# Half of the dense weights narrowed in place during the dense layers, lanes of 108 in the router, and thresholds on ScalarE

## The chip, the cores and the metric

The kernel runs on one core of a Trainium2 chip. Its engines are TensorE (PE, with its weight loads PEld), VectorE (DVE), ScalarE (ACT), GpSimd (Pool) and SyncE (SP), which issues most DMAs. Each engine runs its own instructions in the order written and waits for semaphores. The metric is the device time of one execution in microseconds, lower is better. The kernel is built with every order fixed in the code.

## What is computed

Three stages in a row: an attention that keeps only the scores within `tau` of the row's largest, a mixture of eight experts with one expert per token, and two dense layers whose weights come in float64.

```python
# attention: batch 4, heads 8, 576 tokens, head size 64
scores = scale * q @ k.T
scores = where(scores >= max(scores) - tau, scores, -1e9)
attn = softmax(scores); x = attn @ v                # 2304 x 512 after the heads are joined
# experts: 8 of them, 512 -> 1024 -> 512
logits = x @ w_gate; e = argmax(logits); gate_w = softmax(logits)[e]
eom = sigmoid(x @ w_output_gate)[e]
y[mask of e] = gate_w * eom * (relu(x[mask] @ w1[e]) @ w2[e])
# dense layers: 512 -> 2048 -> 512; w_in and w_out are float64
h = y @ w_in; g = maximum(0.01 * h, h); out = g @ w_out
```

## The kernel before

**Attention** (0 to about 341 us). The work is 16 pairs of heads by nine score tiles of 128 rows x 576. For a tile, PE multiplies (L443), DVE takes the row maximum (`rowmax`, L452), a subtraction gives the threshold `th` = `ntau` - `nm` (L456, on DVE or Pool, as the planner chose), ACT makes the exponential `e` (L462), and DVE masks it, `em` (L470); PE transposes `em` (L499), ACT copies that (`eta`, L228), and PE multiplies by the values (L578). At a pair's start Pool splits the next keys and queries into a high and a low part: two CASTs (L290) and two subtractions (L295). A planner (`pl.add`) lists every step with its cost, what it waits for and a priority made of the tile's number and a weight (`st.w_th` and others); the order that comes out is fixed for each engine.

**Router.** After each batch of tokens, gate logits give the expert of a token (one hot `oh`) and its rank in the expert (`rk`). From rank and expert a table of tokens per expert is inverted on PE: a one-hot row of the rank's low part (`lo`, in lanes of 128) against `sides`, made of the rank's high part (J = 4 groups) and the token number. After the third of four batches `choose` takes the expert with most tokens so far (the star) and gathers its first PRE = 216 tokens; their first layer (L1460) runs at 341 to 354 us, while the last batch is routed. Then `tables` makes the gather list of the largest expert, `fits` sets a flag (L1116), DVE goes on to the lists of the others and the starts in the output, and every engine branches past a spare program for experts that don't fit (L1982, L1983).

**Expert windows** (364 to 623 us). The star's second layer, then the eight experts in order of size, each with a capacity from `CAPS`. All operands are split in a high and a low part and multiplied in three passes. For each, SP loads a quarter of w1 or w2 (512 KB) into one of four buffers `raw` (L1592), ACT casts the high part (L1559), DVE or Pool subtracts for the low part (L1564), PE multiplies (L1661 and L1702), ACT and DVE make the hidden values (L1669, L1675). Tokens come by gathers of 128 rows (L1621) and transposes (L1630).

**Narrowing.** Meanwhile `narrow` turns the float64 weights of the dense layers into float32, in 32 pieces of 128 x 512: a load into `dw`, three integer steps on DVE (L1323, L1329, L1335), an absolute value on ACT (L1341), a fourth DVE step (L1345), and a store of the piece, `cv`, to the DRAM tensor `wf` (L1350).

**Dense layers** (from 623 us). Tokens run in five chunks of up to 512, and within a chunk f = 0 to 15 over blocks of 128 hidden values: `h2` (12 matmuls, L1836) and `out` (12 matmuls, L1862). `act_t` and `act_g` (L1843, L1847) make g in `tg`, which lies in the `dw` buffers, and two steps split it. In the first chunk the weights come back from `wf` as 16 loads of 512 KB into `raw` (L1752) and are split by ACT and by DVE or Pool; later chunks find them in place.

## Time and profile before

| | |
|---|---|
| three runs | 1031.01, 1031.69 (median), 1036.69 us |
| profiled execution | 1034.34 us, its span 1032.6 us |
| PE busy | 982.6 us (95%) |
| DVE, ACT, Pool busy | 658.5, 498.0, 260.2 us |
| moved by DMA | 122.22 MB |

The span is what the profile covers, from the first to the last instruction; the device's time lies a little above it. The profile's numbers are of that one execution. "Busy" is what an engine spends inside instructions. The granted clock is the TensorE clock in tenths or hundredths of full speed; 0.50 and 1.00 are its two levels, 1.2 and 2.4 GHz. An idle time stands with the instruction that ended it, with the releaser behind the arrow.

### The profile page before, as it was taken

How to read it: one execution, taken by the hardware profiler on the slowest of the kernel's cores; microseconds unless marked ns; L12 is line 12 of the kernel's file. 1: busy time of each engine (PE TensorE's matmuls, PEld its weight loads, DVE VectorE, ACT ScalarE, POOL GpSimd, SP SyncE). 2: the span in 40 equal slices, each digit the busy share in tenths (PEclk: the TensorE clock that was granted, in tenths of full speed). 3: DMA queues.
4: the chain of work that ended last, by engine and by line, in shares of the span. 5: the costliest groups of instructions: out<-in, count | busy, mean ns of one | idle time of the engine just before them, and what ended most of it. 6: DMA issues, size and time to landing. Idle time of an engine off the chain costs nothing. (4 is left out here: it accounts for less than half of the span.)

```text
span 1032.6 us, 17029 instructions
## 1 busy us (share of the span) xinstructions
PE 982.6 (95%) x6126; PEld 836.8 (81%) x6126; DVE 658.5 (64%) x1279; ACT 498.0 (48%) x944; POOL 260.2 (25%) x328
## 2 busy tenths in 40 slices
PE   6999999999999799899999999999999999999994
PEld 6777767767776699789999997888888888888884
DVE  7888988898889558998888886533223222322321
ACT  6777767767766255544554644423222322322321
POOL 3533223323211244464337532000100100100000
PEclk9999999999999989899999999999999999999997
DMA  5432423431312597887989877200200200100000
GB/s 140 127 86 71 129 59 85 127 73 41 103 25 96 166 260 261 296 269 241 324 298 320 289 241 232 83 1 12 70 1 1 81 1 1 42 20 1 11 31 22
DMA packets 66876, 122.22 MB, mean 118 GB/s; under 512 B 15776, under 2 KB 33184, under 8 KB 66272
## 3 DMA queue, kind: packets, MB, share of 16 engines
q1 hardware_dynamic: 60368, 100.43, 30.5%
q0 software_dynamic: 6416, 20.63, 7.3%
q8 instruction: 50, 0.82, 0.3%
q14 instruction: 42, 0.34, 0.2%
HBM read 88.39 MB, written 23.31 MB: 108 GB/s over the span
## 5 line engine op out<-in xcount | busy, mean ns | idle before, releaser
L1862 PE MATMUL ps<-arena 128*128 128x512 f32 x864 | 207.4, 390 | 2.3 <-ACT arena L1559 2.3
L1836 PE MATMUL ps<-arena 128*128 128x512 f32 (+1 forms) x960 | 208.1, 368 | 0.0
L1836 PEld LDWEIGHTS ps<-arena 128*128 128x128 f32 x960 | 168.7, 188 | 30.8
L1862 PEld LDWEIGHTS ps<-arena 128*128 128x128 f32 x864 | 161.3, 188 | 35.7 <-ACT arena L1559 2.7
L1847 DVE TENSOR_TENSOR dw<-ps,dw 128x512 f32<-128x512 f32 (+1 forms) x80 | 50.9, 638 | 160.7 <-ACT dw L1843 160.6
L1702 PE MATMUL ps<-arena 128*128 128x216 f32 (+7 forms) x864 | 129.8, 309 | 3.8 <-ACT arena L1669 2.2
L1843 ACT ACTIVATE dw<-ps 128x512 f32<-128x512 f32 (+1 forms) x80 | 44.4, 556 | 183.4 <-PE ps L1836 183.4
L1661 PE MATMUL ps<-arena 128*128 128x400 f32 (+7 forms) x768 | 117.9, 313 | 10.7 <-DVE arena L1675 4.1
L1702 PEld LDWEIGHTS ps<-arena 128*128 128x128 f32 x864 | 124.0, 194 | 4.8 <-ACT arena L1669 2.5
L1661 PEld LDWEIGHTS ps<-arena 128*128 128x128 f32 x768 | 113.9, 194 | 13.6 <-DVE arena L1675 5.1
L452 DVE TENSOR_REDUCE nm<-ps 128x1 f32<-128x576 f32 x144 | 107.0, 753 | 22.4 <-PE ps L443 21.1
L470 DVE SCALAR_TENSOR_TENSOR em<-ps,th,e 128x576 f32<-128x576 f32 x144 | 115.1, 811 | 4.6 <-ACT e L462 2.3
L462 ACT ACTIVATE e<-ps,nm 128x576 f32<-128x576 f32 x144 | 105.7, 749 | 17.0 <-DVE nm L452 12.2
L1891 POOL DMA_INDIRECT out_dram<-sm,oidx x18 | 18.0, 999 | 367.4 <-ACT sm L1885 334.2
L1564 DVE TENSOR_TENSOR arena<-dw,arena 128x512 fp32r<-128x512 f32 (+1 forms) x80 | 52.0, 650 | 91.6 <-PE ps L1862 75.8
L443 PE MATMUL ps<-k,qt 128*128 128x288 f32 x512 | 101.6, 326 | 7.2 <-DVE em L470 6.0
L228 ACT COPY eta<-ps 128x512 f32<-128x512 f32 (+1 forms) x159 | 86.2, 545 | 42.3 <-PE ps L499 41.0
L1559 ACT CAST arena<-raw 128x1024 fp32r<-128x1024 f32 x82 | 84.7, 1048 | 43.1 <-DMA raw<-in_moe_w_dram 33.3
L1564 POOL TENSOR_TENSOR arena<-raw,arena 128x1024 fp32r<-128x1024 f32 x30 | 77.0, 2568 | 82.8 <-ACT arena L1559 69.1
L443 PEld LDWEIGHTS ps<-k,qt 128*128 128x128 f32 x512 | 75.8, 196 | 25.0 <-DVE em L470 10.6
L1564 DVE TENSOR_TENSOR arena<-raw,arena 128x1024 fp32r<-128x1024 f32 x54 | 78.2, 1451 | 26.7 <-ACT arena L1559 21.6
L499 PE MATMUL ps<-ident,em 128*128 128x128 f32 x576 | 89.8, 281 | 1.3 <-DVE em L470 0.7
(236 smaller groups left out, 1161.5 us busy)
## 6 DMA issues: line engine op xcount, KB each, us to landing
raw<-in_moe_w_dram SPq DMA_DIRECT2D x72, 512.0 KB
k<-k POOLq DMA_DIRECT2D x30, 304.0 KB
dw<-in_moe_w_in_dram SPq DMA_DIRECT2D x16, 512.0 KB
wf<-cv SPq DMA_DIRECT2D x32, 256.0 KB
dw<-in_moe_w_out_dram SPq DMA_DIRECT2D x16, 512.0 KB
raw<-wf SPq DMA_DIRECT2D x16, 512.0 KB
rk<-in_k_dram SPq DMA_DIRECT2D x16, 256.0 KB
rq<-in_q_dram SPq DMA_DIRECT2D x16, 256.0 KB
```

Source lines behind the costliest of these rows:

```text
L228: nc.scalar.copy(out=out, in_=in_)
L443: nc.tensor.matmul(out=s[:, c, :], lhsT=lhs, rhs=T[kk, P][:, off + c * HALF:off + (c + 1) * HALF], start=(m == 0), stop=(m == 2 * len(ops) ...
L452: nc.vector.tensor_reduce(out=T["nm", n], in_=T["sc", n], axis=AX.XY, op=ALU.max, negate=True)
L462: nc.scalar.activation(out=T["e", n].rearrange("p (a c) -> p a c", a=2), in_=T["sc", n], func=AF.Exp, bias=T["nm", n][:, 0:1], scale=1.0,)
L470: nc.vector.scalar_tensor_tensor(out=T["em", P, t][:, h, :].rearrange("p (a c) -> p a c", a=2), in0=T["sc", n], scalar=T["th", n][:, 0:1], ...
L499: nc.tensor.transpose(out=bank(o)[:, c * 128:(c + 1) * 128], in_=T["em", P, t][:, h, 64 * h + c * 128:64 * h + (c + 1) * 128], identity=ident,
L1559: nc.scalar.copy(out=out, in_=in_)
L1564: (nc.vector if o.eng == "dve" else nc.gpsimd).tensor_tensor(out=out, in0=in0, in1=in1, op=ALU.subtract)
L1661: nc.tensor.matmul(out=bank(o)[:, 0:n], lhsT=w[:, wi, 128 * f:128 * f + 128], rhs=xx[:, xi, c, :], start=(c == 0 and i == 0), stop=(c == K ...
L1702: nc.tensor.matmul(out=bank(first, d)[:, 0:n], lhsT=w[:, wi, k0:k0 + 128], rhs=hx[:, xi, :], start=(f == 0 and i == 0), stop=(f == 7 and i ...
L1836: nc.tensor.matmul(out=bank(o)[:, 0:n], lhsT=w[:, wi, c, 128 * c2:128 * c2 + 128], rhs=y[:, c, 0:n], start=(k == 0), stop=(k == 3 * KD - 1),)
L1862: nc.tensor.matmul(out=bank(first, t), lhsT=g[:, gi, 128 * t:128 * t + 128], rhs=w[:, wi, c2, :], start=(f == 0 and k == 0), stop=(f == FF ...
```

## The change

Five things change.

1. `narrow` stores only the first 16 pieces (EARLY = 4) to `wf`. The other 16 are loaded, narrowed and, by `late`, split straight from `cv` into the weights' place while the dense layers run: an ACT cast (or DVE), and a subtraction on Pool (15) or DVE (1). `tg` moves from `dw` to `raw`, so that the first `act_t` waits for the split of the last early weight.
2. The router counts ranks in lanes of 108 (LANES) and six groups, and makes its entries batch by batch. `choose` inverts the whole table instead of a copy for the star. The lists of the other experts and the starts are made behind the branch, and gathers of later windows wait for the former.
3. The thresholds run on ACT (85 activations) or Pool (59).
4. CAPS[2] goes from 336 to 324, and windows are gathered in blocks of 108 instead of 128 (25 gathers instead of 23).
5. The priorities of attention and router get new values, which gives a new order on all engines.

```diff
+LANES = PRE // 2
-CAPS = [400, 368, 336, 320, 296, 272, 248, 216]
+CAPS = [400, 368, 324, 320, 296, 272, 248, 216]
+EARLY = 4
...
-                (nc.vector if o.eng == "dve" else nc.gpsimd).tensor_tensor(
-                    out=T["th", n], in0=ntau, in1=T["nm", n], op=ALU.subtract
-                )
+                if o.eng == "act":
+                    nc.scalar.activation(out=T["th", n], in_=T["nm", n], func=AF.Identity, bias=ntau[:, 0:1], scale=-1.0)
+                else:
+                    nc.gpsimd.tensor_tensor(out=T["th", n], in0=ntau, in1=T["nm", n], op=ALU.subtract)
...
-            th = pl.add(("dve", "pool"), (0.07, 0.15), thresh, [m], n + st.w_th, label="th")
+            th = pl.add(("act", "pool"), (0.18, 0.15), thresh, [m], n + st.w_th, label="th")
...
-    J = 4
+    J, JW = 6, 4
...
+        entered = self.entries(pl, b, ranked, one_hot, prio)
         if end:
-            return self.tables(pl, ranked, self.last_cum, self.entries(pl, b, b + 1, ranked, one_hot, prio), prio)
+            return self.tables(pl, self.last_cum, entered, prio)
+        self.before += entered
...
         pt = pl.add("dve", 0.6, parts, [ranked], prio, label="en")
+        hi = pl.add("dve" if end else "pool", 0.4, high, [pt], prio, label="en")
+        out = [pl.add("dve", 0.8, low, [pt], prio, label="en")]
...
-        m = pl.add("dve", 2.0, mine, [s, ranked], pr, label="ch")
-        ls = [pl.add("dve", 0.8, lambda o, b=b: low(o, b), [m], pr, label="ch") for b in range(NB)]
-        p = pl.add("pe", 1.0, mm, [*ls, m], pr, acq=[(bk, 1)], label="ch")
+        p = pl.add("pe", 1.0, lambda o: self.inverse(o, 0, 5 * NB, o, 5 * NB), self.before, pr, acq=[(bk, 1)], label="ch")
...
-        a = add("dve", 0.9, fits, [a])
-        a = add("dve", 1.2, lambda o: tokens(o, 1, E), [a])
-        return add("dve", 1.1, starts, [a])
+        self.others, self.starts = lambda o: tokens(o, 1, E), starts
+        return add("dve", 0.9, fits, [a])
...
-def narrow(pl, nc, dw, cv, w_in, w_out, wf, t0, t1):
+def narrow(pl, nc, dw, cv, w_in, w_out, wf, t0, t1, split):
...
-    for i in range(n):
+    for i in range(n_all):
...
+        if i >= n:
+            split(i, e, a, r_cv, lambda B=B: B["c"].bitcast(F32))
+            continue
...
+    others = pl.add("dve", 1.2, R.others, [], -13, at=free, label="tb")
+    starts = pl.add("dve", 1.3, R.starts, [], 5, at=free, label="tb")
...
-            nt = (n + 127) // 128 if r is not None else 0
+            nt = -(-n // LANES) if r is not None else 0
...
-            g = pl.add("pool", 1.1, gather, [], lead - 8, after=[pool_last], acq=[(r_sm, 1)], dma=0.73, label="gather", at=0.0 if a < 2 else free)
+            g = pl.add("pool", 1.1, gather, [others] if r else [], lead - 8, after=[pool_last], acq=[(r_sm, 1)], dma=0.73, label="gather", at=0.0 if a < 2 else free)
...
+    def late(i, e, a, r_cv, src):
...
+        w = late.when(i)
+        b = pl.add(AD, (0.59, 0.45), hiw, [e, O.get(("wh", k - 1)), *(ends if k >= ar.NW else [prev_hi]), *O.get(("hf", k), [])], w + 0.5,
+                   acq=[(r_w, 1)] if k < ar.NW and half_ == 0 else [], label="wh")
+        l = pl.add(("dve", "pool"), (0.74, 1.4), low, [b], w + 0.6, rel=[(r_cv, a)], label="wl")
...
+    late.when = lambda i: t2 + 10.8 * (i // 4) - 20 + 2.7 * (i % 4)
+    wdone = narrow(pl, nc, dw, cv, w_in, w_out, wf, st.w_n0, t2 - st.w_n1, late)
+    for u in range(NE):
...
-            tt = pl.add("act", ev(n)[0], lambda o, a=a, f=act_t: f(o, a), [a], bf + 3, acq=[(r_t, 1)], label="t")
+            tt = pl.add("act", ev(n)[0], lambda o, a=a, f=act_t: f(o, a), [a, O["wv", 2 * NE - 1]], bf + 3, acq=[(r_t, 1)], label="t")
...
-    st.w_s, st.w_m, st.w_th, st.w_x, st.w_kk, st.w_t, st.w_te = -0.39, -0.27, -4.42, -1.71, -7.74, 2.69, -4.82
+    st.w_s, st.w_m, st.w_th, st.w_x, st.w_kk, st.w_t, st.w_te = -0.83, -9.42, -28.19, 3.88, -7.61, 2.26, -14.75
...
-            st.tg = [t.bitcast(F32).rearrange("p f a -> p (f a)").rearrange("p (a f) -> p a f", a=2) for t in st.dw]
+            st.tg = [t.rearrange("p (a f) -> p a f", a=2) for t in st.raw[2:4]]
```

**ACT in attention.** Before, in the early score tiles, ACT's row holds the exponentials `e` (L462), the copies of the transposed tiles (`eta`, `etl`, L228) and a copy for the output (`xu`):

```order
L228 COPY eta<-ps 128x4x128
L462 ACTIVATE e<-ps,nm 128x576 x2
L228 COPY eta<-ps 128x4x128
L462 ACTIVATE e<-ps,nm 128x576
L228 COPY xu_171<-ps 128x288
L228 COPY etl<-ps 128x384
L228 COPY eta<-ps 128x4x128
L462 ACTIVATE e<-ps,nm 128x576
```

After, in about the same place (exponential L467, copies L232), thresholds stand among them:

```order
L461 ACTIVATE th<-nm,ntau 128x1
L467 ACTIVATE e<-ps,nm 128x576
L232 COPY etl<-ps 128x384
L232 COPY eta<-ps 128x4x128
L467 ACTIVATE e<-ps,nm 128x576
L232 COPY eta<-ps 128x4x128
L467 ACTIVATE e<-ps,nm 128x576
L232 COPY eta<-ps 128x4x128
```

The threshold, made by the same subtraction before on DVE or Pool, now stands ahead of an exponential.

**DVE at the branch.** Before, the flag (L1116) is followed by the gather lists of the other experts (L1103 to L1108) and the sums for the starts:

```order
L1116 TENSOR_SCALAR flag<-mcap 128x1
L1103 TENSOR_TENSOR scr<-one,tab 128x224
L1107 TENSOR_REDUCE tk_4651<-scr 128x28
L1108 TENSOR_SCALAR gidx<-tk_4651 128x28
L1120 TENSOR_TENSOR scr<-gt,cnt 128x64
L1121 TENSOR_REDUCE off<-scr 128x8
L1122 TENSOR_SCALAR off<-off 128x8
L1064 TENSOR_TENSOR scr<-one,off 128x64
```

and the branch stands behind these, the first router steps of the last batch's gate, and the first split of a weight (L1564):

```order
L823 TENSOR_TENSOR d<-lg_4557,m 128x40
L833 TENSOR_TENSOR og<-oh,lg_4557 128x40
L835 TENSOR_REDUCE os<-og 128x5
L1564 TENSOR_TENSOR arena<-raw_66,arena 128x1024
L1982 TENSOR_LOAD flag
L1983 COMPARE_AND_BRANCH
```

After, the comparison with the capacities (L1085 to L1089) ends in the flag and the branch:

```order
L1085 TENSOR_TENSOR scr<-one,capr 128x64
L1086 TENSOR_REDUCE cap<-scr 128x8
L1087 TENSOR_TENSOR dcap<-cnt,cap 128x8
L1088 TENSOR_REDUCE mcap<-dcap 128x1
L1089 TENSOR_SCALAR flag<-mcap 128x1
L1991 TENSOR_LOAD flag
L1992 COMPARE_AND_BRANCH
```

The lists of the others and the starts now stand behind the branch, the lists as the first rows there.

**DVE and PE in the first chunk of the dense layers.** Before, DVE's row there holds the activation's second step (`act_g`, L1847), the split of g (L1564 from `dw`) and splits of weights that came back from `wf` (from `raw`):

```order
L1564 TENSOR_TENSOR arena<-dw_4689,arena 128x512
L1847 TENSOR_TENSOR dw_4690<-ps,dw_4690 128x512
L1561 CAST arena<-raw_68 128x1024
L1564 TENSOR_TENSOR arena<-dw_4690,arena 128x512
L1847 TENSOR_TENSOR dw_4689<-ps,dw_4689 128x512
L1564 TENSOR_TENSOR arena<-dw_4689,arena 128x512
L1564 TENSOR_TENSOR arena<-raw_69,arena 128x1024
L1847 TENSOR_TENSOR dw_4690<-ps,dw_4690 128x512
L1564 TENSOR_TENSOR arena<-dw_4690,arena 128x512
```

After, in the first chunk, the same two steps of the activation (L1856, and L1543 from `raw`) stand between the four narrowing steps of the pieces (L1299, L1305, L1311, L1321):

```order
L1299 TENSOR_SCALAR cv_4688<-dw_4686 128x512
L1305 SCALAR_TENSOR_TENSOR cv_4688<-dw_4686,cv_4688 128x512
L1311 SCALAR_TENSOR_TENSOR cv_4688<-dw_4686,cv_4688 128x512
L1856 TENSOR_TENSOR raw_68<-ps,raw_68 128x512
L1321 SCALAR_TENSOR_TENSOR cv_4688<-dw_4686,cv_4688 128x512
L1543 TENSOR_TENSOR arena<-raw_68,arena 128x512
L1299 TENSOR_SCALAR cv_4689<-dw_4687 128x512
L1305 SCALAR_TENSOR_TENSOR cv_4689<-dw_4687,cv_4689 128x512
L1311 SCALAR_TENSOR_TENSOR cv_4689<-dw_4687,cv_4689 128x512
L1856 TENSOR_TENSOR raw_69<-ps,raw_69 128x512
```

What was four steps per piece during the windows is now, for the last 14 pieces, between the activation steps of f = 0 to 13.

PE, at the start of the same chunk: before, three `h2` (L1836, 12 matmuls each) stand behind the last window (L1702), then `out` (L1862) and `h2` in turn:

```order
L1702 MATMUL ps<-arena 128x216 x96
L1836 MATMUL ps<-arena 128x512 x36
L1862 MATMUL ps<-arena 128x512 x12
L1836 MATMUL ps<-arena 128x512 x12
L1862 MATMUL ps<-arena 128x512 x12
L1836 MATMUL ps<-arena 128x512 x12
```

After, six `h2` (L1845) and then four `out` (L1871) come first:

```order
L1683 MATMUL ps<-arena 128x216 x96
L1845 MATMUL ps<-arena 128x512 x72
L1871 MATMUL ps<-arena 128x512 x48
L1845 MATMUL ps<-arena 128x512 x12
L1871 MATMUL ps<-arena 128x512 x12
L1845 MATMUL ps<-arena 128x512 x12
```

The first `out` moved back by three groups of 12 matmuls.

## Rows read from the trace of the kernel before

**Rows 1.** Page, part 1: busy us, share and instructions of each engine.

```profile
...
PE 982.6 (95%) x6126; PEld 836.8 (81%) x6126; DVE 658.5 (64%) x1279; ACT 498.0 (48%) x944; POOL 260.2 (25%) x328
...
```

**Rows 2.** By stretch, us: length; busy of PE, weight loads, DVE, ACT, Pool; clock; DMA.

```profile
...
180.00:240.00 60.00, 57.53 (x442) 43.89 (x440) 53.46 (x132) 43.03 (x91) 18.77 (x38) 0.97 0.38 92
327.00:341.00 14.00, 12.49 (x124) 7.99 (x122) 9.40 (x26) 7.34 (x19) 5.80 (x12) 1.00 0.18 59
354.00:378.00 24.00, 17.69 (x115) 16.61 (x116) 14.50 (x23) 10.89 (x21) 13.04 (x8) 0.79 0.79 183
414.00:455.00 41.00, 36.62 (x205) 35.86 (x205) 39.44 (x55) 19.80 (x32) 20.96 (x13) 0.92 0.79 268
455.00:490.00 35.00, 32.69 (x203) 32.10 (x204) 30.85 (x33) 17.28 (x29) 16.02 (x8) 0.95 0.79 263
640.00:720.00 80.00, 80.00 (x355) 66.24 (x354) 34.08 (x44) 29.32 (x45) 1.03 (x1) 1.00 0.14 43
...
```

**Rows 3.** Waits of PE, whole span: us in total, times, longest.

```profile
...
PE ps L443 <- DVE em L470: 6.0, 5, 2.3
...
PE ps L1661 <- DVE arena L1675: 4.1, 4, 2.3
PE ps L1661 <- ACT arena L1559: 3.6, 1, 3.6
PE ps L1661 <- DVE arena L1564: 2.3, 2, 1.4
PE ps L1862 <- ACT arena L1559: 2.3, 1, 2.3
...
```

**Rows 4.** The threshold line L456 on DVE: duration in ns, min/median/max.

```profile
...
L456 DVE TENSOR_TENSOR th<-ntau,nm x47: 147/159/4007, 15.0 to 276.9; 128x1 f32<-128x1 f32 x47
...
```

**Rows 5.** Timeline, all engines, 131 to 138 us: start, duration, engine, line, operation.

```profile
...
131.68 4.01 DVE L456 TENSOR_TENSOR th<-ntau,nm 128x1 f32<-128x1 f32 x1
...
134.25 1.41 POOL L295 TENSOR_TENSOR srq<-rq,srq 128x576 fp32r<-128x576 f32 x1
...
```

**Rows 6.** By stretch, three pieces in which the granted clock is down; columns as rows 2.

```profile
...
137.50:140.90 3.40, 3.40 (x14) 2.38 (x15) 3.37 (x10) 2.34 (x4) 0.00 (x0) 0.50 0.46 59
219.40:222.80 3.40, 3.27 (x12) 2.50 (x14) 3.21 (x11) 1.79 (x3) 0.00 (x0) 0.50 0.60 51
417.40:424.20 6.80, 5.86 (x18) 5.48 (x19) 6.63 (x6) 3.93 (x6) 5.45 (x3) 0.50 0.95 311
...
```

**Rows 7.** Timeline, all engines, 397 to 406 us, early in the windows.

```profile
...
399.20 5.27 POOL L1564 TENSOR_TENSOR arena<-raw,arena 128x1024 fp32r<-128x1024 f32 x2 [5.89 <-ACT arena L1559]
399.34 2.85 DVE L1335 SCALAR_TENSOR_TENSOR cv<-dw,cv 128x512 int32<-128x512 int32 x1
...
404.94 0.41 DVE L1323 TENSOR_SCALAR cv<-dw 128x512 int32<-128x512 int32 x1
...
405.39 0.69 DVE L1329 SCALAR_TENSOR_TENSOR cv<-dw,cv 128x512 int32<-128x512 int32 x1
...
```

**Rows 8.** Lines by shape, 364 to 630 us: busy us, mean ns; idle before, releasers.

```profile
...
L1564 POOL TENSOR_TENSOR arena<-raw,arena 128x1024 fp32r<-128x1024 f32 x29 | 74.0, 2556 | 70.5 <-ACT arena L1559 69.1 <-remote 1.2
...
L1345 DVE SCALAR_TENSOR_TENSOR cv<-dw,cv 128x512 f32<-128x512 f32 x32 | 35.7, 1117 | 6.6 <-ACT dw L1341 5.3
L1335 DVE SCALAR_TENSOR_TENSOR cv<-dw,cv 128x512 int32<-128x512 int32 x32 | 34.6, 1080 | 0.4
L1329 DVE SCALAR_TENSOR_TENSOR cv<-dw,cv 128x512 int32<-128x512 int32 x32 | 29.7, 928 | 0.5
...
L1323 DVE TENSOR_SCALAR cv<-dw 128x512 int32<-128x512 int32 x32 | 18.5, 577 | 3.9 <-DMA dw<-in_moe_w_out_dram 2.5 <-DMA dw<-in_moe_w_in_dram 1.4
...
```

**Rows 9.** A small ACT activation, line L838: duration in ns, min/median/max.

```profile
...
L838 ACT ACTIVATE os<-os x4: 203/216/217, 130.5 to 354.2; 128x5 f32<-128x5 f32 x4
...
```

**Rows 10.** Timeline, all engines, 349.5 to 360 us, around the branch.

```profile
...
349.92 0.15 DVE L1116 TENSOR_SCALAR flag<-mcap 128x1 int32<-128x1 f32 x1
...
359.55 0.35 ACT L1669 ACTIVATE arena<-ps 128x216 fp32r<-128x216 f32 x1 [4.24 <-DVEq L1983]
...
```

273 lines of the change are left out of this document (130 added, 143 removed).

## The prediction

> **What bounds the kernel now.** I read the engine totals first: TensorE (PE) is busy 982.6 of 1032.6 us [rows 1], so the time can fall only where PE idles, where its clock is down, or where it has less to do. Part of the 50 idle us lies at the start and the end, which the change leaves alone. The table by stretch [rows 2] shows where else: little in attention, 1.5 of 14 us in its tail, 6.3 of 24 us where the program branches into the expert windows, 4.4 of 41 and 2.3 of 35 us early in the windows; the dense layers from 640 us have none (80.00 of 80.00). The list of PE's waits [rows 3] names who ended them: VectorE's (DVE's) masked scores `em` 6.0 us, then DVE and ScalarE (ACT) splitting weights or hidden values.
>
> Two waits, near 132 and 214 us, have one cause. The threshold `th`, a subtraction of two columns, takes 159 ns at the median on DVE but 4007 at most [rows 4]. The instance at 131.68 ends 0.03 us behind a subtraction of GpSimd (Pool), the last of four operations that split a pair's keys and queries there [rows 5]; PE then waits up to 2.3 us [rows 3]. The clock rows show a second price: after each of the two waits PE runs 3.4 us at a granted clock of 0.50 (1.2 of 2.4 GHz), and 6.8 us after the long wait at 414 us [rows 6]. PE is busy in those, so half of such a stretch is lost.
>
> The windows show the same: a narrowing step at 399.34 takes 2.85 us under two Pool subtractions, its undisturbed neighbours 0.41 and 0.69 [rows 7]. The means of the four narrowing steps [rows 8], less 0.41 and three times 0.69, leave 0.167 + 0.238 + 0.390 + 0.427 = 1.22 us of hold per piece, 39 us for 32 pieces. Beside 29 Pool subtractions of 2.56 us that is 1.35 us for each, about half its length.
>
> **Attention: thresholds to ACT.** Of 144, 47 ran on DVE [rows 4] and none does now, so the two long holds lose their victim: 2 x 2.3 idle and 2 x 1.7 of clock, 8 us. In their place 85 small activations go to ACT (the other 59 stay with Pool) at about 0.22 us each (the nearest row is a 5-column activation [rows 9]): 18.7 us on an engine busy 43 of 60 us there [rows 2], hence some 48 of 60. In the order shown one stands right ahead of the exponential that the mask also waits for, so each can lengthen the chain of its tile by 0.2 us; I charge 1 us in all, since the ring of score tiles gives slack. The other side: all priorities of attention are new, and each batch's lane tests (`low`, two SBUF inputs, 128x640) now run on DVE during attention. If three of them meet a Pool run as `th` did, they bring back 3 x (2.3 + 1.7) = 12 us. Value: -7; bounds -9 and +5.
>
> **Tail and branch.** The choice of the star expert drops nine small DVE steps and three lane tests from the tail, where PE idles 1.5 us [rows 2]: -1 (0 to -2.7). The flag was ready at 349.92 + 0.15, but DVE then made the other gather lists, the starts and one split before it branched, and ACT's first relu behind the branch stood at 359.55, after 4.24 us whose end is put down to DVE's branch [rows 10]. Now DVE branches right behind the flag. What is late next is ACT's own branch, and then the other gather lists, 1.3 us on DVE behind the branch, with all gathers of later windows behind them on Pool. Of the 6.3 idle and the clock of 0.79 (5 us of 24) I take -2; bounds 0 and -6.
>
> **Windows.** The first 16 pieces are stored as densely as before, so up to about 490 us DVE carries what it carried (39.4 of 41 us [rows 2]). There PE lost 4.4 + 2.3 us idle and, by the clocks of 0.92 and 0.95 [rows 2], 3.3 + 1.7, and I expect a fifth of this back, from other alignment: -2. Behind 490 the narrowing is gone from DVE, ACT and the DMA queues. The 4.1 + 3.6 + 2.3 = 10.0 us that PE waits in the windows [rows 3] less those 6.7 leave 3.3, of which 3 should go. Sum -5; bounds 0 and -14. CAPS[2] takes 192 matmuls x 12 columns away: at 355 matmuls of 512 columns in 80 us [rows 2], 0.44 ns a column, that is 1.0 us; two more transposes by four, of 128 columns, give 0.5 back: -0.5.
>
> **Dense layers.** The 2.3 us wait for the first `out` [rows 3] should go: what came late was a read back of `wf`, and the eight that are left were stored long before. The first relu now waits for the split of the last early weight, which waits for two output stores of the last window; I put it at 6 us after the dense start (t2), and the fifth `h2` needs its bank at t2 + 10.8: covered by 4 us. So -2.3.
>
> The late pieces cost. One group of 12 matmuls takes 12 x 80 / 355 = 2.7 us [rows 2]. PE runs 6 `h2`, 4 `out`, then alternates, so `h2`(14), which needs pieces 28 and 29, starts after 26 groups, at t2 + 70.3; `h2`(12) at 59.5, `out`(12) at 72.9, `out`(14) at 81. By DVE's order piece 20 begins behind about 10 activation steps of 0.7 us and two pieces of 2.5 that cannot start before t2 + 6; I take t2 + 20. From there stand 12 pieces x 2.48 = 29.8 us [rows 7] and 21 steps of 0.69 (two splits or products for each `f`) = 14.5: 44.3 us, 3.7 per piece. Pool subtracts one half tile per piece, half of 2.56 us; by the half found above it holds DVE 0.67 each: 4.4 per piece. Ten pieces then end at t2 + 64, and with ACT's and Pool's split behind them 66: in time. But DVE has 10 `f` of 5.4 us for it, and needs 5.2 of each: no room for bunching, and a late product holds a bank of `h2`. I charge one wait of 1.5 us with its 1.7 of clock: +3. Net +1; bounds -2.3 and +8.
>
> Half of Pool's time is what the rows show as hold, and 4.01 us for a step of 0.16 [rows 4, 5] shows that it can be all of it. The Trainium skill, "SBUF — State Buffer", section "SBUF: two separate sides", has the harder rule: DVE and GpSimd share a port pair that is locked for a whole instruction, and a DVE instruction with two SBUF inputs fully blocks against a GpSimd one that reads SBUF. By it, with DVE always asking, each Pool subtraction here costs its whole 1.28 us, 5.0 per piece; `h2`(14) would be 1.3 us late, and the sum 3 to 4 us higher.
>
> **Sum.** -7 - 1 - 2 - 5 - 0.5 + 1 = -14.5. The profiled execution took 1034.34 us (span 1032.6), 2.65 above the median 1031.69; so 1019.8 for a run like it, 1017.2 by the median: 1017, with 1011 to 1024 for this case.
>
> **Rivals.** (a) *DVE in the dense layers sets the end.* For: 16 pieces where PE has no idle time today, and DVE nearly full by my count. The point is 4.8 us per piece; at 5.4, where each Pool subtraction costs DVE its whole 1.28 us and 0.4 more, `h2`(14) is 6 us late, with the clock 8: dense +8 in place of +1, 1024. It doesn't end above before by itself.
>
> (b) *The new order of attention makes PE wait: slower.* Place: score matmuls waiting for `em`, now five waits of 6.0 us in all [rows 3], 1.2 each. ACT is asked for the exponential, the copies and 85 thresholds, and a threshold behind a copy of 0.6 us delays the mask of its tile. For: DVE busy 53 of 60, both engines in order. Against: the score tiles stand in rings, and ACT would still idle some 12 of 60 us. Price: one such wait per pair of heads, 16 x 1.2 = 19 us, in place of -7: 1043. The other terms give 7.5 back: it decides the sign from 0.5 us per pair on, and is slower by over 0.5% from 0.8 on.
>
> (c) *The holds only change their victim.* Pool still runs its CASTs and subtractions, and DVE's lane tests and router steps with two SBUF inputs stand at the same places. Then attention gives 0, the tail 0, the branch -1, the windows -2.5, the dense layers +3: 1031, no change.
>
> (d) *More goes than I count.* The windows' waits all go with their clock (-14) and the branch gives -5: about 1005.
>
> **How the numbers follow.** Forecast 0.50, (a) 0.10, (b) 0.14, (c) 0.16, (d) 0.10. Faster or slower means by over 0.5% (5.2 us), about what a measurement of this kernel can tell from no change. Forecast, (a) and (d) are faster, 0.70 together, less 0.02 for ends of (a) above 1026.5: 0.68; no change 0.18 with them; slower 0.14. The range from 1004 to 1034 leaves out (b) and a twentieth at the lower end.
>
> **What would show it.** Right: no DVE step over 3 us in attention, no half-clock stretch near 140 and 220 us; DVE out of the branch by 356; no PE wait over 0.5 us between 490 us and the dense start; no wait of `out` there; narrowing steps up to 2 us between t2 + 10 and t2 + 75, and PE waits of at most 3 us among them. Wrong: PE waits for `em` totalling over 15 us (b), lane tests or router steps of 3 to 4 us (c), `h2` or `out` of f = 10 to 15 waiting for weights for over 5 us (a).

## The result, and the profile after

The changed kernel takes 1018.19 us (median of four runs, 1016.2 to 1020.31), the kernel before 1031.35 beside it: ratio 0.9866, 95% interval 0.9822 to 0.9911. The forecast was 1017, range 1004 to 1034, faster. The profiled execution of the changed kernel took 1020.31 us with a span of 1018.5, that of before 1034.34 with 1032.6.

The engine totals, to be read beside [rows 1]; PE (TensorE) is still the bound:

```profile
...
PE 978.2 (96%) x6134; PEld 834.6 (82%) x6134; DVE 648.4 (64%) x1255; ACT 512.5 (50%) x1022; POOL 253.2 (25%) x304
...
```

PE's waits, to be read beside [rows 3] (us in total, times, longest):

```profile
...
PE ps L1642 <- ACT arena L1538: 6.2, 2, 5.7
...
PE ps L1611 <- DMA sm<-xrows,gidx: 3.1, 1, 3.1
PE ps L1642 <- DVE arena L1656: 2.6, 1, 2.6
PE ps L1642 <- DVE arena L1543: 2.4, 2, 1.9
...
PE ps L447 <- DVE em L475: 1.0, 1, 1.0
...
```

The masked scores (`em`) fell from 6.0 to 1.0 us, the first `out` doesn't appear any more. What grew is the wait for ACT's casts of high parts (L1538), from 3.6 to 6.2, and there is a new one of 3.1 for a token gather behind the branch.

The stretches that answer to [rows 2] (length; busy time of PE, weight loads, DVE, ACT, Pool; clock; DMA share and GB/s):

```profile
...
180.00:240.00 60.00, 59.83 (x464) 45.26 (x462) 53.75 (x134) 48.08 (x111) 20.84 (x36) 1.00 0.36 97
346.00:370.00 24.00, 18.37 (x125) 17.45 (x125) 17.09 (x28) 11.33 (x22) 9.48 (x9) 0.79 0.69 225
405.00:447.00 42.00, 34.36 (x195) 33.86 (x195) 40.19 (x66) 20.72 (x33) 20.21 (x13) 0.88 0.75 255
480.00:512.00 32.00, 29.44 (x194) 29.02 (x193) 26.50 (x32) 16.01 (x27) 13.56 (x7) 0.95 0.87 302
541.00:567.00 26.00, 26.00 (x210) 25.80 (x209) 15.56 (x21) 12.13 (x21) 16.15 (x14) 1.00 0.64 207
...
628.00:700.00 72.00, 72.00 (x319) 59.61 (x318) 62.19 (x82) 32.93 (x56) 19.94 (x14) 1.00 0.30 88
...
```

Attention is full (59.83 of 60, clock 1.00), the branch has not changed (18.37 of 24, clock 0.79, before 17.69), early windows lose more than before (34.36 of 42 at a clock of 0.88), later ones nothing (26.00 of 26), and in the first chunk of the dense layers DVE is busy 62.19 of 72 us while PE never waits.

To put places to the 14.1 us of span, this table has the first matmul of each stage in the timeline of each profiled execution, and the lengths between: L1 is the star's first layer, W the first window of 400, D the first `h2`. The last column is the time at half clock between W and D.

```
kernel                     L1     W      D      end   | L1..W  W..D   D..end | half
before                   340.9  377.5  622.9  1032.6  |  36.6  245.4  409.7  | 10.2
after                    333.6  368.5  611.3  1018.5  |  34.9  242.8  407.2  | 13.7
e1_before_th_act         342.0  379.1  628.1  1037.9  |  37.1  249.0  409.8  |  6.8
e2_after_th_dve          336.2  370.5  612.1  1019.3  |  34.2  241.7  407.2  | 10.2
e3_all_by_dram           333.2  367.9  621.2  1028.4  |  34.7  253.4  407.2  | 17.1
e4_no_pool_in_windows    333.1  367.2  607.4  1014.6  |  34.2  240.2  407.1  | 10.2
e5_early2                333.7  367.1  606.7  1023.2  |  33.3  239.7  416.5  |  6.8
e6_lists_before_flag     332.5  368.0  607.0  1014.1  |  35.5  239.0  407.2  | 10.2
e7_narrow_later          333.2  367.0  599.7  1008.8  |  33.8  232.7  409.1  |  0.0
e8_after_old_prio        335.5  369.2  607.9  1015.0  |  33.7  238.7  407.2  |  3.4
e9_all_by_dram_spread    333.2  367.1  611.3  1019.5  |  33.9  244.1  408.2  | 10.2
e10_no_pool_spread       332.8  367.2  593.6  1000.7  |  34.4  226.4  407.2  |  0.0
e11_best                 332.9  367.3  593.7  1000.9  |  34.4  226.4  407.2  |  0.0
e12_all_by_dram_ties     334.0  369.0  619.5  1026.6  |  35.0  250.5  407.2  | 17.1
```

Between the two kernels -7.3 us fall to L1, -1.7 to the branch, -2.6 to the windows and -2.5 to the dense layers. One execution is a poor ruler for the windows: before and e1 have the same code there and differ by 3.6 us, and after, e2, e6 and e8, whose windows are edited alike, lie between 238.7 and 242.8. Taken over all of these, before is at 247.2 and after at 240.5, so the pair shows less of the windows' gain than there is.

### The profile page after: what moved, and what is told of

The parts are those of the page before. It is cut to its first block, busy times and chain, and to the rows that moved or that the text cites. A ratio compares the mean times of both kernels' runs of the same rounds, so it can differ in the third digit from the quotient of the medians.

```text
span 1018.5 us, 16995 instructions
## 1 busy us (share of the span) xinstructions
PE 978.2 (96%) x6134; PEld 834.6 (82%) x6134; DVE 648.4 (64%) x1255; ACT 512.5 (50%) x1022; POOL 253.2 (25%) x304
## 5 line engine op out<-in xcount | busy, mean ns | idle before, releaser
L1845 PE MATMUL ps<-arena 128*128 128x512 f32 (+1 forms) x960 | 207.6, 368 | 0.0
L1871 PE MATMUL ps<-arena 128*128 128x512 f32 x864 | 206.7, 389 | 0.0
L1543 DVE TENSOR_TENSOR arena<-raw,arena 128x512 fp32r<-128x512 f32 (+2 forms) x135 | 133.1, 990 | 112.2 <-PE ps L1871 67.1
L1845 PEld LDWEIGHTS ps<-arena 128*128 128x128 f32 x960 | 168.7, 188 | 30.8
L1538 ACT CAST arena<-raw 128x1024 fp32r<-128x1024 f32 (+2 forms) x155 | 123.2, 806 | 131.9 <-PE ps L1871 57.9
L1871 PEld LDWEIGHTS ps<-arena 128*128 128x128 f32 x864 | 161.4, 188 | 33.0
L1856 DVE TENSOR_TENSOR raw<-ps,raw 128x512 f32<-128x512 f32 (+1 forms) x80 | 50.6, 636 | 135.4 <-ACT raw L1852 135.2
L456 DVE TENSOR_REDUCE nm<-ps 128x1 f32<-128x576 f32 x144 | 108.7, 755 | 20.5 <-PE ps L447 17.6
L1852 ACT ACTIVATE raw<-ps 128x512 f32<-128x512 f32 (+1 forms) x80 | 44.1, 555 | 152.4 <-PE ps L1845 152.4
L467 ACT ACTIVATE e<-ps,nm 128x576 f32<-128x576 f32 x144 | 106.7, 742 | 2.5 <-DVE nm L456 2.5
L447 PE MATMUL ps<-k,qt 128*128 128x288 f32 x512 | 104.6, 329 | 1.3 <-DVE em L475 1.0
L232 ACT COPY eta<-ps 128x512 f32<-128x512 f32 (+1 forms) x157 | 83.5, 544 | 25.2 <-PE ps L504 25.0
L504 PE MATMUL ps<-ident,em 128*128 128x128 f32 x576 | 85.4, 276 | 0.8 <-DVE em L475 0.8
L583 PE MATMUL ps<-eta,rv 128*64 128x288 f32 x512 | 83.8, 425 | 0.6 <-ACT k L232 0.5
L504 PEld LDWEIGHTS ps<-ident,em 128*128 128x128 f32 x576 | 68.1, 141 | 4.9 <-ACT e L467 2.6
```

The costliest lines, as they stand in the source:

```text
L447: nc.tensor.matmul(out=s[:, c, :], lhsT=lhs, rhs=T[kk, P][:, off + c * HALF:off + (c + 1) * HALF], start=(m == 0), stop=(m == 2 * len(ops) ...
L456: nc.vector.tensor_reduce(out=T["nm", n], in_=T["sc", n], axis=AX.XY, op=ALU.max, negate=True)
L467: nc.scalar.activation(out=T["e", n].rearrange("p (a c) -> p a c", a=2), in_=T["sc", n], func=AF.Exp, bias=T["nm", n][:, 0:1], scale=1.0,)
L504: nc.tensor.transpose(out=bank(o)[:, c * 128:(c + 1) * 128], in_=T["em", P, t][:, h, 64 * h + c * 128:64 * h + (c + 1) * 128], identity=ident,
L583: nc.tensor.matmul(out=out[64 * h:64 * h + 64], lhsT=T["rv", P][:, 4 * h + c, :], rhs=T["eta", P][:, h, c, lo_:lo_ + HALF], start=(c == 0) ...
L1538: nc.scalar.copy(out=out, in_=in_)
```

## The experiments

### Attention: thresholds, priorities, or router

**The kernel before with the thresholds on ACT**

```diff
-                (nc.vector if o.eng == "dve" else nc.gpsimd).tensor_tensor(
-                    out=T["th", n], in0=ntau, in1=T["nm", n], op=ALU.subtract
-                )
+                if o.eng == "act":
+                    nc.scalar.activation(out=T["th", n], in_=T["nm", n], func=AF.Identity, bias=ntau[:, 0:1], scale=-1.0)
+                else:
+                    nc.gpsimd.tensor_tensor(out=T["th", n], in0=ntau, in1=T["nm", n], op=ALU.subtract)
...
-            th = pl.add(("dve", "pool"), (0.07, 0.15), thresh, [m], n + st.w_th, label="th")
+            th = pl.add(("act", "pool"), (0.18, 0.15), thresh, [m], n + st.w_th, label="th")
```

> The kernel before with part 3 of the change alone: thresholds on ACT or Pool, old priorities. Theory H (the held thresholds on DVE cost 8 us): no threshold step above 0.4 us, no half-clock stretch near 140 and 220 us, the star's first layer starts at 333 to 336 us in place of 340.9, and the time falls by 5 to 8 us, to 1024 to 1027. Rival P (the gain of attention is that of the new priorities): the old order has no place for 0.3 us steps on ACT, PE waits for the masked scores grow, the first layer starts at 339 to 345, time 1029 to 1035.

It took 1036.27 us, ratio 1.0017 (0.9991 to 1.0043): no gain. The holds went, as theory H said: there is no half-clock stretch near 140 or 220 us, and the 481st of 640 score matmuls starts at 246.2 us in place of 250.5. But from there to L1 it takes 95.8 us in place of 90.4: the 4.3 us were lost again, and 1.1 more. The lines of thresholds on ACT (count, busy us, mean ns) and two of PE's waits in the tail:

```profile
...
L457 ACT ACTIVATE th<-nm,ntau 128x1 f32<-128x1 f32 x62 | 18.5, 298 | 11.6 <-DVE nm L452 9.5 <-DVE ria L926 1.9
...
```

```profile
...
325.77 1.32 PE L443 MATMUL ps<-k,qz 128*128 128x288 f32 x8 [1.40 <-DVE ias L1028]
...
330.37 0.47 PE L536 MATMUL ps<-ident,em 128*128 128x128 f32 x1 [0.74 <-POOL em L527]
...
```

PE waits 1.40 us for `ias`, the index that `choose` makes for the star's tokens, then 0.74 us for a copy, and runs 6.8 us at half clock near 327 us. The old `choose`, with its long chain on DVE, stands there; in the kernel before the same chain costs less. A threshold on ACT is 0.298 us, not the 0.22 estimated.

**The changed kernel with the thresholds on DVE or Pool**

```diff
-            th = pl.add(("act", "pool"), (0.18, 0.15), thresh, [m], n + st.w_th, label="th")
+            th = pl.add(("dve", "pool"), (0.07, 0.15), thresh, [m], n + st.w_th, label="th")
```

> The changed kernel with part 3 undone: thresholds on DVE or Pool again, new priorities. Theory H: one or two threshold steps of about 4 us on DVE under the Pool run of a pair's split, each with a PE wait of about 2.3 us and a half-clock stretch of 3.4 us; the star's first layer starts at 337 to 342 us in place of 333.6, time 1022 to 1027. Rival P: it starts at 332 to 335, time 1016 to 1020.

It took 1019.98 us, ratio 0.9859 (0.9806 to 0.9913), the same as the changed kernel. Thresholds on DVE (ns, min/median/max):

```profile
...
L460 DVE TENSOR_TENSOR th<-ntau,nm x64: 141/152/1412, 14.2 to 319.9; 128x1 f32<-128x1 f32 x64
...
```

The longest is 1412 ns; none of the 64 met a whole Pool run. The 481st score matmul starts at 242.9 us, in the changed kernel at 243.3. So with the new priorities DVE is as good a place as ACT in the middle of attention; L1 starts 2.6 us later. Theory H expected holds that weren't there.

**The changed kernel with the old priorities**

```diff
-    st.w_k = [-9.01, -41.3, -10.8, -7.75, -2.8]
-    st.w_s, st.w_m, st.w_th, st.w_x, st.w_kk, st.w_t, st.w_te = -0.83, -9.42, -28.19, 3.88, -7.61, 2.26, -14.75
+    st.w_k = [-8.06, -12.57, -8.02, -7.15, -5.65]
+    st.w_s, st.w_m, st.w_th, st.w_x, st.w_kk, st.w_t, st.w_te = -0.39, -0.27, -4.42, -1.71, -7.74, 2.69, -4.82
...
```

> The changed kernel with part 5 alone undone: the priorities of the kernel before, thresholds on ACT or Pool. Theory P (the new priorities carry the gain of attention, since the thresholds on ACT gained nothing in the kernel before): the star's first layer starts at 338 to 343 us in place of 333.6, time 1023 to 1029. Rival R (the router's new split into batches carries it): it starts at 333 to 336, time 1017 to 1021.

1017.09 us, ratio 0.9839 (0.979 to 0.9888): rival R, the router. L1 starts at 335.5, with the same priorities and ACT thresholds but the old router (e1) at 342.0. PE's waits up to 342 us:

```profile
...
PE ps L323 <- ACT eta L232: 1.4, 2, 1.1
...
PE ps L447 <- DVE em L475: 0.9, 3, 0.5
...
```

They are many and small. The 481st score matmul starts at 246.3 us, as in e1 (246.2); from there to L1 it is 89.2 us, in e1 95.8. So with thresholds on ACT and the old priorities the batch-wise router is worth 6.5 us, all of it in the last part of attention. But the kernel before, with the old router, needs 90.4 us for that part: the new router keeps what e1 lost rather than adding 6.5 us. The new priorities are worth 1.9, and the thresholds' place, which I had put first, between +1.1 (before to e1) and -2.6 (e2 to after), depending on the order around it. These are single executions; in the ten with the attention of the changed kernel L1 starts between 332.5 and 334.0 us.

### The branch

**Lists and starts ahead of the flag's branch again**

```diff
-        self.others, self.starts = lambda o: tokens(o, 1, E), starts
-        return add("dve", 0.9, fits, [a])
+        a = add("dve", 0.9, fits, [a])
+        self.others = a = add("dve", 1.2, lambda o: tokens(o, 1, E), [a])
+        self.starts = starts
+        return add("dve", 1.1, starts, [a])
...
-    others = pl.add("dve", 1.2, R.others, [], -13, at=free, label="tb")
-    starts = pl.add("dve", 1.3, R.starts, [], 5, at=free, label="tb")
+    others = starts = None
```

> The changed kernel with the gather lists of the other experts and the starts made ahead of the branch again. Theory B (the branch was late for DVE's work behind the flag): the first window of 400 starts 1.5 to 2.5 us later than at 368.5, time 1019 to 1021. Rival G (what is late there is the gather or ACT): within 0.5 us of 368.5, time 1017 to 1019.

1017.73 us, ratio 0.985 (0.9819 to 0.9881): by the time, rival G. W stands at 368.0; from L1 it is 35.5 us, within 0.6 of the changed kernel, where kernels with an equal branch spread from 33.3 to 35.0. DVE in the changed kernel, flag and first row behind the branch:

```profile
...
343.78 0.16 DVE L1089 TENSOR_SCALAR flag<-mcap 128x1 int32<-128x1 f32 x1
349.75 0.57 DVE L1076 TENSOR_TENSOR scr<-one,tsa 128x224 f32<-128x224 f32 x1 [5.81 <-DVEq L1992]
...
```

The flag is done at 343.9, and DVE goes on 5.8 us later, with no other row between: so long is the branch. In e6 PE waits first for the gather, as in the changed kernel, and then for ACT:

```profile
...
348.29 0.56 PE L1612 MATMUL ps<-ident,sm 108*128 108x108 f32 x4 [3.24 <-DMA sm<-xrows,gidx]
351.21 0.55 PE L1684 MATMUL ps<-arena 128*128 128x216 f32 x1 [2.36 <-ACT arena L1651]
...
```

Its first matmul of the star's second layer (351.21) comes 6.2 us behind the end of L1, in the changed kernel 4.0 (350.18 behind 346.2). So theory B holds at that place, with 2.2 us: the kernel before has 6.0 us there and e1 6.9, the eleven executions that branch right behind the flag 3.8 to 4.4. W comes only 0.6 later than in the changed kernel (1.3 later than the mean of the eleven, 34.2 us from L1), and the total shows nothing. The edit brings back the lists and the starts alone; the router steps and the split of a weight that also stood ahead of the branch before stay behind it.

### Narrowing late, or by way of DRAM

**All pieces by DRAM**

```diff
-EARLY = 4
+EARLY = 8
...
-            tt = pl.add("act", ev(n)[0], lambda o, a=a, f=act_t: f(o, a), [a, O["wv", 2 * NE - 1]], bf + 3, acq=[(r_t, 1)], label="t")
+            tt = pl.add("act", ev(n)[0], lambda o, a=a, f=act_t: f(o, a), [a], bf + 3, acq=[(r_t, 1)], label="t")
...
-            st.tg = [t.rearrange("p (a f) -> p a f", a=2) for t in st.raw[2:4]]
+            st.tg = [t.bitcast(F32).rearrange("p f a -> p (f a)").rearrange("p (a f) -> p a f", a=2) for t in st.dw]
```

> The changed kernel with EARLY = 8: all 32 pieces narrowed in the windows and brought back from DRAM as before, the activation's scratch in the dw buffers again; the rest of the change stays. Theory N (narrowing half of the pieces late is worth 4 to 5 us, in the second half of the windows and at the dense start, and costs nothing in the dense layers): PE waits between 490 us and the dense start come back with 2 to 4 us, the first out waits about 2 us again, time 1020 to 1025. Rival M (the late pieces cost in the dense layers what they give before): 1016 to 1019.

It took 1029.52 us, ratio 0.9951 (0.9923 to 0.9979): more than theory N expected. PE's waits:

```profile
...
PE ps L1642 <- DVE arena L1656: 9.6, 4, 4.1
...
PE ps L1642 <- issue: 3.8, 5, 1.3
...
```

Waits for hidden values (L1656) are 9.6 us, and 3.8 us have no releaser ("issue"); these, and a 4.1 us wait among the former, stand at 569 to 583 us, when Pool issues 17 gathers of single values (`mt`) in a row. The dense layers are as long as in the changed kernel (407.2). To see whether that is a property of the program, it ran again, unchanged (the label says more than was edited):

> e3_all_by_dram once more, for one look. Theory F (its run of 17 Pool gathers of single values, unbroken, starves all engines of instructions near 570 to 583 us, 7 us of PE idle and 10 us of half clock): the same waits without a releaser near the same gathers, span 1027 to 1030. Rival Q (a chance event of one execution): none of them, span 1015 to 1020.

One execution, 1021.28 us: no wait without a releaser, D at 611.3 in place of 621.2, although the same 17 gathers stand in a row at 561 to 585 us. The waits for hidden values alone are 6.2 us:

```profile
...
PE ps L1642 <- DVE arena L1656: 6.2, 4, 1.8
...
```

**The same with the gathers moved behind the windows**

```diff
-        mts.append(pl.add("pool", 1.1, weight, [oi, last, pool_last], t2 + 2 * j, dma=0.3, label="mt"))
+        mts.append(pl.add("pool", 1.1, weight, [oi, last, pool_last, O["wv", min(j, 15)]], t2 + 2 * j, dma=0.3, label="mt"))
```

> e3_all_by_dram with the 18 gathers of single values (mt) tied one by one to the splits of the dense weights, so that they don't stand in one run in the windows. Theory F (what e3 lost beyond 2 us was instructions held up by that run): no PE wait without a releaser in the windows, dense layers from 609 to 613, time 1016 to 1021, so that narrowing half of the pieces late is worth 0 to 3 us by itself. Theory N (the late narrowing itself is worth 10 us): dense layers from 617 to 622, time 1025 to 1030.

1024.52 us, ratio 0.9895 (0.9871 to 0.9919), between the ranges of both. No wait without a releaser is left in the windows (15 gathers run in a row at 616 to 638 us, in the dense layers, and PE doesn't wait there); those for hidden values stay:

```profile
...
PE ps L1642 <- DVE arena L1656: 8.6, 7, 2.8
...
```

With all pieces by DRAM the windows take 253.4, 244.1 and 250.5 us. The first of these has the waits near the gathers in it; the other two have a mean of 247.3, as the kernel before and e1 (247.2), against 240.5 in the four executions with half of them late. The execution with 250.5 was the slowest of six, 3.9 us above their median, so that 6.8 us is too much; by the ratios (0.9895 here, 0.9839 to 0.9866 in the changed kernel, e2, e6 and e8, with intervals that overlap) it is 3 to 6 us. So narrowing half of the pieces late gives some 3 to 7 us, between the two theories, and costs the dense layers nothing that the trace shows. It isn't why they got 2.5 us shorter: they are at 407.2 to 408.2 with all pieces by DRAM too, and the first `out` waits at most 0.8 us there.

**Three quarters late**

```diff
-EARLY = 4
+EARLY = 2
```

> The changed kernel with EARLY = 2: 24 of the 32 pieces narrowed late. Theory D (in the dense layers DVE needs about 4.4 us per late piece and PE uses one per 2.7 us, so 16 late pieces are near the limit): DVE is over 95% busy from the dense start on, h2 and out wait for weights for 15 to 30 us in all, time 1033 to 1046. Rival E (late pieces are cheap, since their steps fill DVE's idle time and many can be done before the dense start): PE waits below 5 us, time 1014 to 1022.

1023.88 us, ratio 0.9903 (0.9871 to 0.9935): neither. The windows are 3.1 us shorter than in the changed kernel, the dense layers 9.3 longer. PE's waits from 606 to 720 us, and the stretches from D to 705:

```profile
...
PE ps L1871 <- ACT arena L1538: 6.3, 4, 2.1
PE ps L1845 <- POOL arena L1543: 0.6, 1, 0.6
```

```profile
...
606.70:660.00 53.30, 53.30 (x237) 44.16 (x237) 50.80 (x69) 27.96 (x49) 18.41 (x13) 1.00 0.41 130
660.00:705.00 45.00, 37.93 (x159) 28.91 (x158) 39.76 (x53) 22.01 (x37) 13.85 (x11) 1.00 0.29 91
...
```

DVE is 95% busy from D to 660, as theory D said, and from `out`(11) on PE waits for weights, 6.9 us of the 9.3 by which the stage is longer. But the delay is smaller than it counted; the trace suggests why, though no run tests it: the plan had `h2` and `out` alternate from the start, and pieces come one per 4.2 us (Pool's 24 splits, from 2.6 us after D for the third to 91.7 for the last). The limit is between 16 and 24 late pieces.

### What holds the windows

**No Pool subtraction in the windows**

```diff
-                *((("dve", "pool"), (1.5, 2.7)) if r is not None else ("dve", 1.4)), lambda o, f=lo, ld=ld, h=a: f(o, ld, h), [a], need - 11.9, rel=[(r_raw, ld)], label="lo", at=free)
+                *("dve", 1.4), lambda o, f=lo, ld=ld, h=a: f(o, ld, h), [a], need - 11.9, rel=[(r_raw, ld)], label="lo", at=free)
```

> The changed kernel with all low parts of the windows' weights on DVE, none on Pool. Theory K (Pool's subtractions hold DVE, and that blocks the stores and the loads behind them, so that PE waits 5.7 and 1.9 us near 405): no narrowing step above 1 us before the dense start, DVE busy about the same in the windows although it does 21 subtractions of 1.2 us more, PE's wait near 405 below 3 us, time 1010 to 1016. Rival W (what is late there is DVE's work itself, or the loads): the wait stays at 5 to 9 us or grows, time 1017 to 1026.

The lines of DVE, first of the changed kernel from 333 to 611 us, then of this one from 333 to 607 (count, busy us, mean ns):

```profile
...
L1543 DVE TENSOR_TENSOR arena<-raw,arena 128x1024 fp32r<-128x1024 f32 x52 | 75.2, 1455 | 18.3 <-ACT arena L1538 16.8 <-PE ps L1642 1.1
L1321 DVE SCALAR_TENSOR_TENSOR cv<-dw,cv 128x512 f32<-128x512 f32 x18 | 19.3, 1074 | 1.1 <-ACT arena L1650 0.5
...
```

```profile
...
L1543 DVE TENSOR_TENSOR arena<-raw,arena 128x1024 fp32r<-128x1024 f32 x72 | 87.1, 1226 | 32.3 <-ACT arena L1538 26.8 <-issue 4.7 <-PE ps L1642 0.6
L1321 DVE SCALAR_TENSOR_TENSOR cv<-dw,cv 128x512 f32<-128x512 f32 x18 | 12.4, 687 | 0.5
...
```

All but one of Pool's subtractions are gone, and every step is at its undisturbed length: 1226 ns for a split (1455 before), 687 for the last narrowing step (1074). DVE makes 72 splits in place of 52 and needs 87 us for them in place of 75; what it saves on the narrowing and the rest is more. Two stretches of this kernel:

```profile
...
405.00:447.00 42.00, 41.38 (x260) 40.99 (x259) 38.16 (x72) 20.82 (x35) 13.43 (x7) 1.00 0.85 302
549.00:564.00 15.00, 9.31 (x42) 7.72 (x41) 1.23 (x1) 2.33 (x4) 9.04 (x10) 0.72 0.31 104
...
```

The first is what theory K expected: 41.38 of 42 us where the changed kernel has 34.36, DVE 38.16 for 40.19. Yet the time is 1016.8 us, ratio 0.9842 (0.9792 to 0.9891), outside K's range, because of the second stretch: PE 9.31 of 15, everything else nearly still, clock 0.72. There Pool issues its 18 `mt` gathers from 536 to 560 without a break. Three of PE's rows, and what the DMA engines moved from 549 to 564 us (GB/s in 40 equal slices):

```profile
...
555.43 0.48 PE L1683 MATMUL ps<-arena 128*128 128x272 f32 x2 [0.91 <-issue]
...
560.41 1.10 PE L1642 MATMUL ps<-arena 128*128 128x248 f32 x4 [0.91 <-issue]
562.54 1.87 PE L1642 MATMUL ps<-arena 128*128 128x248 f32 x8 [1.02 <-issue]
```

```profile
...
GB/s 131 186 262 251 284 339 404 383 383 411 377 269 171 131 88 33 2 0 0 2 0 0 0 1 0 0 2 44 0 0 1 0 0 2 0 0 0 0 0 15
...
```

**The same with the gathers spread over the dense layers**

```diff
-        mts.append(pl.add("pool", 1.1, weight, [oi, last, pool_last], t2 + 2 * j, dma=0.3, label="mt"))
+        mts.append(pl.add("pool", 1.1, weight, [oi, last, pool_last, O["hl2", 8 + min(j, 15) // 2][min(j, 15) % 2]], t2 + 2 * j, dma=0.3, label="mt"))
```

> e4_no_pool_in_windows with the 18 gathers of single values (mt) tied one by one to the late pieces' splits in the dense layers, so that no run of them stands in the windows. Theory F: PE's waits of 4 us near 552 to 562 and the half clock of 10 us behind them go, the dense layers start at 597 to 600 in place of 607.4, time 1007 to 1011. Rival Q: they stay or were chance, the dense layers start at 604 to 608, time 1014 to 1018.

1004.66 us, ratio 0.972 (0.9672 to 0.9768). The windows are 13.8 us shorter than in e4, with no half clock, and PE never waits in them:

```profile
...
405.00:447.00 42.00, 42.00 (x267) 41.91 (x266) 38.12 (x73) 21.07 (x36) 12.90 (x7) 1.00 0.86 303
...
541.00:593.00 52.00, 52.00 (x455) 52.00 (x454) 28.22 (x39) 22.96 (x41) 2.39 (x1) 1.00 0.59 191
...
```

**Narrowing from later on, Pool's subtractions as they were**

```diff
-    st.w_n0, st.w_n1 = 30, 30
+    st.w_n0, st.w_n1 = 90, 30
```

> The changed kernel with the start of the narrowing set 60 us later in the plan, so that the first window's end near 405 us has none. Theory S (the narrowing, held by Pool, keeps the stores on SP waiting and the weight loads behind them): the waits of 5.7 and 1.9 us near 405 fall below 2 us together, and waits of a similar kind may come where the narrowing now starts, time 1010 to 1018. Rival L (the loads are late for the DMA queues' own rate): 5 to 8 us of wait near 405 stay, time 1017 to 1021.

1012.72 us, ratio 0.9804 (0.9772 to 0.9837): the waits fall as theory S said, though not by way of SP (see below). Near 405 us 1.7 of 7.7 us of wait are left, no half clock in the windows; one wait of 2.1 comes near 503, and an `out` waits 1.3 in the dense layers:

```profile
...
400.00:430.00 30.00, 28.31 (x170) 27.68 (x169) 21.08 (x41) 14.17 (x23) 9.18 (x8) 1.00 0.53 188
500.00:540.00 40.00, 37.10 (x292) 35.97 (x291) 34.79 (x50) 20.56 (x38) 16.41 (x10) 1.00 0.86 295
...
```

**All three**

```diff
-                *((("dve", "pool"), (1.5, 2.7)) if r is not None else ("dve", 1.4)), lambda o, f=lo, ld=ld, h=a: f(o, ld, h), [a], need - 11.9, rel=[(r_raw, ld)], label="lo", at=free)
+                *("dve", 1.4), lambda o, f=lo, ld=ld, h=a: f(o, ld, h), [a], need - 11.9, rel=[(r_raw, ld)], label="lo", at=free)
...
+        mts.append(pl.add("pool", 1.1, weight, [oi, last, pool_last, O["hl2", 8 + min(j, 15) // 2][min(j, 15) % 2]], t2 + 2 * j, dma=0.3, label="mt"))
...
-    st.w_n0, st.w_n1 = 30, 30
+    st.w_n0, st.w_n1 = 90, 30
```

> Three of the edits together: narrowing 60 us later, no Pool subtraction in the windows, the mt gathers spread over the dense layers. If the gains add up: PE waits below 2 us between 400 us and the dense start, dense layers from 595 to 599, time 1004 to 1009. If DVE becomes the bound behind 430 us: waits of 3 us and more there, time 1010 to 1015.

1003.0 us, ratio 0.9704 (0.9656 to 0.9752), the fastest: 30.8 us under the kernel before. The stages are those of e10 to 0.2 us, so without Pool's subtractions it no longer matters when the narrowing starts: two edits, not three, do the work.

## Why the prediction was right, and where it wasn't

**Attention and tail, -7 and -1: -7.3 came, where it was forecast, but only in part by the step that was priced.** By the 481st of 640 score matmuls the changed kernel is 7.2 us ahead (243.3 against 250.5); from there to L1 both take the same (90.3 and 90.4), so the tail gave nothing in the pair. The holds of [rows 4, 5] are real, and taking the thresholds off DVE in the old order removed them (e1, e8): it gave 4.2 to 4.3 us by that matmul. The rest, 3.0, came with the new order (e8 to the changed kernel), which I held for a risk. In that order the thresholds on DVE meet no long hold either (e2). The step that was mis-sized is "two long holds lose their victim", 8 us: I priced a stall by what it costs where it stands, and didn't ask what was late next. In e1 that was the index for the star, and the whole gain was lost; the new router, which I had priced at -1, keeps it (e8). What the new router gives by itself stays open, since no run has it with the old thresholds and the old order. The 12 us of new holds that I feared didn't come: DVE's longest step before 333 us takes 1.37 us, and there is no half-clock stretch in attention.

**Branch, -2: -1.7 came, by the cause that was named.** DVE's work behind the flag was late: with part of it back (e6), PE's first matmul behind the branch comes 2.2 us later, which is what the kernel before has (6.0 us behind L1's end, 6.2 in e6, 4.0 in the changed kernel). To the first window 0.6 to 1.3 us of it are left. What stands next isn't ACT's own branch, as I wrote: the branch itself takes 5.8 us, and PE then waits 3.1 us for a token gather.

**Windows, -5 and -0.5: -2.6 in the pair, -6.7 over six executions.** That behind 490 the waits go was right: 541 to 567 has 26.00 of 26. That the early ones stay was right too, and they grew to 5.70 + 1.95 us near 405. The prediction has the first link of their chain, the hold; the trace shows the others:

```profile
...
402.48 2.38 POOL L1543 TENSOR_TENSOR arena<-raw,arena 128x1024 fp32r<-128x1024 f32 x1 [2.00 <-ACT arena L1538]
402.62 2.79 DVE L1321 SCALAR_TENSOR_TENSOR cv<-dw,cv 128x512 f32<-128x512 f32 x1
...
405.79 0.69 DVE L1305 SCALAR_TENSOR_TENSOR cv<-dw,cv 128x512 int32<-128x512 int32 x1
...
406.54 0.34 SPq L1571 DMA_DIRECT2D raw<-in_moe_w_dram  x1
406.56 0.67 ACT L1317 ACTIVATE dw<-dw 128x512 f32<-128x512 f32 x1 [4.17 <-DVE cv L1305]
407.13 1.03 ACT L1538 CAST arena<-raw 128x1024 fp32r<-128x1024 f32 x1
...
408.48 2.00 ACT L1538 CAST arena<-raw 128x1024 fp32r<-128x1024 f32 x2
...
410.37 0.30 ACT L1538 CAST arena<-ps 128x176 fp32r<-128x176 f32 x1
...
410.73 0.68 PE L1642 MATMUL ps<-arena 128*128 128x368 f32 x1 [5.70 <-ACT arena L1538]
```

A Pool subtraction starts at 402.48. DVE's last step of one piece, begun 0.14 us after it, ends at 405.4 with 2.79 us in place of 0.69, and so the next piece's second step ends only at 406.5. ACT stands still for 4.17 us until then, because that piece's absolute value (L1317) is next in its row. Behind it come casts of weights without a gap, and last the high part of the window's last 44 tokens (128x176), which ends at 410.7 and lets PE go. The 1.95 us wait ends with the low part of the same tokens on DVE, behind a split that takes 2.54 us beside the Pool subtraction of 409.62. The SP queue, which I suspected in the expectations of e4 and e7, isn't the way: the store does wait for DVE, but the weight load of 406.54 lands at 413.9, after PE has gone on. The kernel before has the same pattern (PE 3.58 us at 417, the 3.6 of [rows 3], ended by tokens and not by a weight; ACT 3.94 us at 406). That the hold is the cause is shown: e4 takes the Pool subtractions away, e7 the narrowing, and in both ACT's stop near 405 and all but 0.6 and 1.7 us of the wait there are gone. How much of the 5.70 us each link costs isn't shown, since the loads and splits before 402 were held in the same way.

**Dense layers, +1: -2.5.** The sizes of the late pieces were right. DVE's four narrowing steps and Pool's subtraction from 611 us on:

```profile
...
L1543 POOL TENSOR_TENSOR arena<-cv,arena 128x512 fp32r<-128x512 f32 x15 | 21.8, 1451 | 62.5 <-ACT arena L1538 62.5
...
L1305 DVE SCALAR_TENSOR_TENSOR cv<-dw,cv 128x512 int32<-128x512 int32 x14 | 13.6, 971 | 0.4
...
L1311 DVE SCALAR_TENSOR_TENSOR cv<-dw,cv 128x512 int32<-128x512 int32 x14 | 11.6, 828 | 0.3
L1321 DVE SCALAR_TENSOR_TENSOR cv<-dw,cv 128x512 f32<-128x512 f32 x14 | 10.5, 750 | 0.6
...
L1299 DVE TENSOR_SCALAR cv<-dw 128x512 int32<-128x512 int32 x14 | 9.2, 660 | 0.0
...
```

The steps' means sum to 3.21 us, 0.72 over their undisturbed 2.49, beside Pool subtractions of 1.45: half, as estimated from [rows 8] (0.67). From the split of piece 20 to that of piece 31 it is 49.1 us in the timeline, 4.46 per piece, against 4.4. Piece 29 is split at 67.5 us after D (forecast 66), `h2`(14) starts at 70.8. So the wait of 1.5 us with its clock that I charged for "bunching" had no row, and wasn't there. The Trainium skill, "SBUF — State Buffer", section "SBUF: two separate sides", lets the loser wait for the whole instruction; by that, with DVE always asking, a piece would take 5.0 us. A single step does wait that long (402.62 above), but over many the measured hold is half of Pool's time. The 2.3 us wait of the first `out` went, as forecast, but not for fewer reads back: e3 and e12 have all sixteen and no such wait. In the kernel before it ended with ACT's cast of the first g, which stood right behind the cast of a read-back that waited 2.86 us for its load; in e3 and e12 that g stands ahead of the next such cast. By these rows it is ACT's order that took the wait away there; no run tests it.

**Rivals.** (a) is shown where it was not asked, at 24 late pieces. (b) didn't come: `em` is 1.0 us; nearest to it is e1, whose order wasn't fitted to thresholds on ACT and which isn't faster than before. (c) didn't. (d)'s 1005 was there to be had, from two other edits.

So the sum came out close, within 0.4 us of the spans (-14.1 for -14.5) and 1.3 us of the medians, by luck: +2.9 in the windows and -3.5 in the dense layers met, and in attention 8 us for the holds, which gave 4.3, met 3.0 from a new order that was priced as a risk. The direction rested on firmer ground: each of the kernels that undo one part (e2, e3, e6, e8, e12) stays under the kernel before.
